# The place of every PSUM tile written in the source: a table of banks in place of two buffer counts

## The chip, the core and the metric

The kernel runs on one core of one Trainium2 chip. The number that counts is its time on the device in microseconds (us); three runs of the kernel before are at hand, and their median is the time to which the changed kernel is compared. Beside them stands one execution taken by the hardware profiler, with a row for every instruction of five engines: TensorE (PE in the profile, its weight loads apart as PEld), VectorE (DVE), ScalarE (ACT), GpSimd (POOL) and SyncE (SP), which issues the DMAs. "Span" is the time from the first to the last instruction of that execution.

## What is computed

A linear-attention recurrence with a decay per channel, and behind it a feed-forward layer with the larger of two projections. Cut to what matters:

```python
# r, k, v, w: (4, 8, 768, 48);  u: (8, 48)
for t in range(S):
    cur = einsum('bhd,bhe->bhde', u[None] * kt, vt)
    y[:, :, t] = einsum('bhd,bhde->bhe', rt, state + cur)
    state = wt[:, :, :, None] * state + einsum('bhd,bhe->bhde', kt, vt)
x = y.transpose(0, 2, 1, 3).reshape(3072, 384)
g = maximum(x @ w1, x @ w2)          # 384 -> 1024
out = g @ w_out                      # 1024 -> 384, float32
```

## The kernel before

**Tiling.** The 768 steps are cut into three segments of 256 tokens, and the eight units are batches of such segments: units 0 to 3 are one batch each of the first segment, units 4 and 5 two batches each of the second, 6 and 7 two batches each of the third. Inside a segment the recurrence becomes matrix products: a key-query score tile for each of two halves, masked, times the values; the state that a segment leaves is carried into the next.

**Order.** Nothing is scheduled by a tool. A string `ORDER` lists 652 short steps, each naming a function, its unit and parts, and after an `@` the engine; the kernel walks through it and records each step's instructions. Every engine then runs its own instructions in that order, and an instruction starts when those ahead of it on its engine have been issued and the semaphores that it waits for have been raised. A wait at the head of an engine's queue holds back all that is behind it.

**The steps that matter here.** In a step's name the first number is the unit.

- `sc` (function `sc`, matmuls at L641): scores of a batch and half, into a pair of PSUM banks. `mk` (L650, VectorE) reads them through the mask into the bf16 tile `M`.
- `ya` (L688) and `yi` (L675): masked scores times values, and state times queries, summed into one pair for a batch. `xe` (copy helper at L168) takes that pair out to `xT`.
- `kv` (L596): the segment's new state, into a pair; `st` (L612, L615, VectorE) reads it. It needs `kp` from `scale` (multiplications by the helpers L176 on VectorE, L180 on GpSimd) and `vp` from `vb` (L168).
- `ex` (L395 to L398): prefix sums of the logarithms, into a bank; `e0` (L436, ScalarE) takes the exponential in place, and `scale` reads it. `ie` (L460, ScalarE) makes the inverse factors `iE`.
- `gt` (L706): one eighth of the 1024 hidden channels for a unit, into a bank; `rl` (L717 on ScalarE, L719 on VectorE) writes them out as `gT`.
- `op` (L725 for the folded part, L729 for the rest): 128 output rows into a bank; `oe` copies them out, `os` (L743) stores them.
- `dt` (L582): DMA transposes of `rp` and `kp` into `RK`, from which `sc` reads. `load` (L372): loads of r, k, v, w.

**PSUM.** It has eight banks of 2 KiB on each partition. Tag `G` has four of them (each tile one bank; 113 tiles in the program), tag `Y` has the other four as two pairs (44 tiles). Which of the four banks, or of the two pairs, a tile gets is left to the pool: it has a number of buffers for each tag and hands one out when the tile is made. The first write to a tile has to wait until the last reader of the tile that had the place before is done, so the place decides for whom TensorE waits.

```python
BANKS = {'G': 4, 'Y': 2}
```

Around the place of which most is said below, `ORDER` reads (units 4 to 7 mixed):

```
mz.6.1 e0.6.1 ie.6.0 kw.6.0@d e0.6.0 scale.6.1.1.0@p di.5.1@d sc.5.1.0.0
ya.5.0.1.0 rw.6.0@d ya.5.0.0.0 yi.5.0 xe.5.0@a vb.6.0@a scale.6.0.0.0@d op.4.2 wl.5 os.3.1
scale.6.1.0.0@p sc.5.1.1.0 oe.4.2@a op.4.0 oe.4.3@a oe.4.0@a mk.5.1.0.0 wp.7.0@p ya.5.1.0.0
mk.5.1.1.0 dt.6.0.0 ya.5.1.1.0 yi.5.1 kv.6 scale.6.0.1.0@d dt.6.0.1 xe.5.1@d st.6.0 dt.6.1.1 ln.7.0
```

## Time and profile before

| | before |
|---|---|
| three runs, us | 146.37, 147.02, 146.45 |
| their median, us | 146.45 |
| the profiled execution's span, us | 147.2 |
| mean granted TensorE clock in it | 0.987 |
| VectorE busy, us | 116.9 (79%) |
| ScalarE busy, us | 90.6 (62%) |
| GpSimd busy, us | 90.0 (61%) |

The profiled execution has no time of its own beside its span, and that span is longer than each of the three runs. Durations below are from this one execution. In rows of the timeline the first number is the start in us from the start of the span, the second the time from the first start to the last end of the merged instructions, then come engine, line, operation, the tile written and the tiles read; what stands in brackets is how long the engine was idle just before, and who ended that.

### The profile page before, as it was taken

The numbers are of one execution on the slowest core, as the hardware profiler recorded it, in microseconds if no ns is written. First come the engines' busy times: TensorE is split into PE (matmuls) and PEld (weight loads), VectorE is DVE, ScalarE is ACT, GpSimd is POOL, SyncE is SP. The second block draws the span as 40 slices with busy tenths as digits, with TensorE's granted clock in tenths as the row PEclk, the third lists the DMA queues.
The fourth block names the chain that finished last, engine by engine and source line by source line (L and its number), as shares of the span: only waits on it lengthen the run. The fifth ranks groups of instructions, "written<-read, shape, count | busy, mean of one in ns | idle before, by whom it ended". The sixth has DMA issues, their size and how long they took to land.

```text
span 147.2 us, 5536 instructions
## 1 busy us (share of the span) xinstructions
PE 136.8 (93%) x2403; PEld 84.2 (57%) x2404; DVE 116.9 (79%) x162; ACT 90.6 (62%) x164; POOL 90.0 (61%) x106
## 2 busy tenths in 40 slices
PE   5999999779999999999999994999999999999990
PEld 1355755568757666875654562554557545664560
DVE  2489999999999999999999967399967589361511
ACT  4053793997999849999178677367357483227010
POOL 7659979996986299499785909506996900000000
PEclk9999999999999999999999999599999999999999
DMA  4999999999899899997978999799933990051014
GB/s 104 323 325 357 335 401 394 366 286 304 214 241 277 212 226 282 312 255 174 205 192 177 292 251 207 141 138 291 250 136 78 131 271 20 0 210 62 4 56 157
DMA packets 71186, 31.84 MB, mean 216 GB/s; under 512 B 66293, under 2 KB 70390, under 8 KB 71162
## 3 DMA queue, kind: packets, MB, share of 16 engines
q1 hardware_dynamic: 71162, 31.49, 81.2%
q8 instruction: 19, 0.31, 0.8%
q14 instruction: 5, 0.04, 0.2%
HBM read 23.61 MB, written 4.73 MB: 193 GB/s over the span
## 4 chain that ended last, share of the span: by engine, by line
PE 41%; DVE 35%; issue 6%; POOL 6%; DMA 4%; ACT 3%; SPq 2%; DVEq 0%; POOLq 0%; ACTq 0%
PE G L729 12%; DVE M L650 9%; PE G L706 8%; PE G L234 7%; PE G L725 5%; DVE rp L176 4%; DMA lv<-in_v_dram 4%; DVE rku L176 3%; DVE dg L502 3%; POOL kp L180 3%; DVE M L516 3%; PE Y L688 2%; SPq L582 2%; POOL rku L180 2%; PE Y L675 2%
## 5 line engine op out<-in xcount | busy, mean ns | idle before, releaser
L729 PE MATMUL G<-wo_sb,gT 128*128 128x384 bf16 x192 | 35.8, 331 | 0.0
L706 PE MATMUL G<-xT,wd_sb 128*128 128x256 bf16 (+1 forms) x192 | 34.4, 326 | 0.7 <-ACT xT L168 0.6
L650 DVE CAST_PREDICATED M<-mask,Y 128x1024 bf16<-128x1024 int32 (+1 forms) x26 | 28.6, 1131 | 2.8 <-PE Y L641 1.9
L717 ACT ACTIVATE gT<-G 128x512 bf16<-128x512 f32 x43 | 24.5, 601 | 9.8 <-PE G L706 9.6
L729 PEld LDWEIGHTS <-gT 128*128 128x128 bf16 x192 | 19.0, 99 | 12.6 <-issue 0.3
L706 PEld LDWEIGHTS <-wd_sb 128*128 128x128 bf16 x192 | 17.9, 98 | 12.6 <-DVE wd_sb L176 0.6
L180 POOL TENSOR_TENSOR kp<-lk,iE 128x384 bf16<-128x384 f32 x16 | 17.1, 1096 | 9.3 <-DVE lk L176 4.2
L725 PE MATMUL G<-wc_sb,xT 128*128 128x384 bf16 x72 | 15.7, 327 | 0.0
L180 POOL TENSOR_TENSOR rku<-rku,u_b 128x384 f32<-128x384 f32 x14 | 14.5, 1053 | 2.0 <-DVE rku L176 2.0
L234 PE MATMUL G<-S_b 128*128 128x512 bf16 x47 | 13.6, 442 | 1.8 <-DVE S_b L263 1.8
L168 ACT COPY RK<-G 128x1024 bf16<-128x1024 bf16 x12 | 12.1, 1019 | 4.7 <-PE G L565 4.7
L168 ACT COPY osb<-G 128x384 f32<-128x384 f32 x7 | 3.4, 479 | 15.9 <-PE G L729 12.6
L180 POOL TENSOR_TENSOR rku<-lr,lk 128x384 f32<-128x384 f32 x8 | 10.9, 1393 | 2.5 <-DMA lk<-in_k_dram 1.7
L641 PE MATMUL Y<-RK 48*64 48x128 bf16 x384 | 9.0, 220 | 2.6 <-DVE M L650 2.4
L502 DVE TENSOR_REDUCE dg<-rku 128x16 f32<-128x768 f32 x12 | 11.0, 945 | 0.1
L641 PEld LDWEIGHTS <-RK 48*64 48x64 bf16 x384 | 6.2, 106 | 7.8 <-issue 6.7
L168 ACT CAST xT<-Y 128x768 bf16<-128x768 f32 x7 | 7.0, 1025 | 5.3 <-PE Y L675 4.0
L168 ACT CAST S_b<-S_f 64x768 bf16<-64x768 f32 (+1 forms) x14 | 8.7, 624 | 2.3 <-DVE S_f L612 2.0
L176 DVE TENSOR_TENSOR rp<-lr,G 128x768 bf16<-128x768 f32 (+2 forms) x11 | 8.8, 799 | 1.4 <-ACT G L436 1.4
L234 PEld LDWEIGHTS <-S_b 128*128 128x128 bf16 x48 | 5.1, 112 | 8.3 <-issue 3.3
L516 DVE TENSOR_TENSOR M<-identq,gd 128x512 int32<-128x512 int32 x12 | 9.2, 778 | 0.4 <-POOL gd L168 0.3
L168 DVE CAST xT<-Y 128x768 bf16<-128x768 f32 x5 | 5.1, 1017 | 5.5 <-PE Y L688 3.2
(111 smaller groups left out, 240.2 us busy)
## 6 DMA issues: line engine op xcount, KB each, us to landing
lk<-in_k_dram SPq DMA_DIRECT2D x12, 384.0 KB, 4.7
lv<-in_v_dram SPq DMA_DIRECT2D x12, 384.0 KB, 5.8
lr<-in_r_dram SPq DMA_DIRECT2D x10, 384.0 KB, 5.5
lw<-in_w_dram SPq DMA_DIRECT2D x9, 384.0 KB, 5.4
out_dram<-osb SPq DMA_DIRECT2D x14, 192.0 KB, 3.9
gT<-in_moe_w_dram SPq DMA_DIRECT2D x4, 512.0 KB, 8.3
out_dram<-wb SPq DMA_DIRECT2D x10, 192.0 KB, 2.0
wso<-in_moe_w_out_dram SPq DMA_DIRECT2D x4, 384.0 KB, 5.5
```

What stands on the lines that cost most here:

```text
L168: (nc.scalar.copy if e == "a" else nc.vector.tensor_copy if e == "d" else nc.gpsimd.tensor_copy)(o, i)
L176: op(o, a, b)
L180: op(o[:, g], a[:, g], b[:, g])
L234: nc.tensor.matmul(t, zz[:, 0:P], zz[:, 0:512], start=True, stop=True)
L502: nc.vector.reduce_sum(s.dg[:, b].rearrange("p i h -> p h i"), s.rku[:, b], axis=AX.X)
L516: (nc.vector if en == "d" else nc.gpsimd).tensor_tensor(out=o, in0=m, in1=g.unsqueeze(3).to_broadcast([P, 2, H, Q // 2]), op=ALU.bitwise_and)
L641: nc.tensor.matmul(t[q * Q:(q + 1) * Q, e, p * P:(p + 1) * P].rearrange("s (i g) -> s i g", i=2), s.kT[d, b, j, y * n + p, q, :], s.rT[d, ...
L650: nc.vector.copy_predicated(t[:, :, 2 * n * y:2 * n * (y + 1)].rearrange("s i (p e) g -> s p e i g", e=2), mask[:, j].bitcast(I32).unsquee ...
L706: nc.tensor.matmul(t[:, m * n * P:(m + 1) * n * P].rearrange("c (b t) -> c b t", t=P), wd_sb[:, ko, fo * P:(fo + 1) * P], s.xT[:, 0:n, ko, :],
L717: nc.scalar.activation(o, i, AF.Relu)
L725: nc.tensor.matmul(t[:, 0:HD], s.xT[:, a, ko, :], wc_sb[:, ko, :], start=(ko == 0), stop=False)
L729: nc.tensor.matmul(t[:, 0:HD], s.gT[:, c:c + P], wo_sb[:, f, :], start=False, stop=(f == FO - 1))
```

## The change

The two buffer counts go, and a table takes their place: one digit for each tile, in the order in which the tiles are made. A digit says which of four banks (`G`) or of two pairs (`Y`) the tile gets, by making the tag `G0` to `G3` or `Y0`, `Y1`, each with a single buffer. By the table, a new tile gets the place whose last user stands earliest in `ORDER`. No step, no instruction and no engine's order is changed; the source grows by nine lines above the steps, so each line number after them is larger by nine.

```diff
-BANKS = {'G': 4, 'Y': 2}
+PLACES = {
+    'G': ("0123013112032303031020230130230210323102121320123013021021023120121310231013021321302131"
...
+    'Y': ("01001010010101010110010010011010101101011001"),
+}
...
+    places = {tag: iter(x) for tag, x in PLACES.items()}
+
+    def place(tag):
+        return tag + next(places[tag])
+
     def bank(dt=F32, tag="G"):
-        return ps.tile([P, 512 if dt is F32 else 1024], dt, tag=tag, name=tag, bufs=BANKS[tag])
+        return ps.tile([P, 512 if dt is F32 else 1024], dt, tag=place(tag), name=tag, bufs=1)

     def pair(tag="Y"):
-        return ps.tile([P, 2, 512], F32, tag=tag, name=tag, bufs=BANKS[tag])
+        return ps.tile([P, 2, 512], F32, tag=place(tag), name=tag, bufs=1)
```

Names of banks aside, most tiles follow the same tile as before on their place. Another one goes before them at 21 of the 157 tiles. Four of these are pairs: `sc.5.0.1.0` and `kv.5`, then `sc.5.1.1.0` and `ya.5.1.0.0`. The seventeen banks are those of `gt.1.3`, `gt.0.2`, `gt.0.3`, `ex.3.0`, `gt.3.0`, `gt.2.3`, `op.3.0`, `op.3.1`, `gt.5.4`, `gt.5.6`, `gt.6.5`, `gt.6.3`, `gt.6.6`, `gt.6.0`, `gt.6.1`, `op.6.0` and `op.6.2`. In the built program the only thing that moves is for whom TensorE's instructions wait (and one instruction of ScalarE waits for a later one of its own engine, ahead of it in the same queue).

The first place is on TensorE, unit 5 and the output of unit 4: `Y_2196` is the pair of `sc.5.1.1.0`, `G_2215` the bank of `op.4.0`, `Y_2235` the pair of `ya.5.1.0.0`. Before:

```order
L729 MATMUL G_2179<-wo_sb_87,gT_1870 128x384
L641 LDWEIGHTS RK_1678
L641 MATMUL Y_2196<-RK_1678 64x128 [waits DVE_49]
...
L725 LDWEIGHTS xT_1815
L725 MATMUL G_2215<-wc_sb_88,xT_1815 128x384 [waits Activation_49]
...
L688 LDWEIGHTS vp0_76
L688 MATMUL Y_2235<-M1_81,vp0_76 32x128 [waits Activation_49]
```

The same place of the changed program:

```order
L738 MATMUL G_2179<-wo_sb_87,gT_1870 128x384
L650 LDWEIGHTS RK_1678
L650 MATMUL Y_2196<-RK_1678 64x128 [waits Activation_49]
...
L734 LDWEIGHTS xT_1815
L734 MATMUL G_2215<-wc_sb_88,xT_1815 128x384 [waits DVE_49]
...
L697 LDWEIGHTS vp0_76
L697 MATMUL Y_2235<-M1_81,vp0_76 32x128 [waits DVE_49]
```

`sc.5.1.1.0` had the pair of `sc.5.1.0.0` and so waited for VectorE's `mk.5.1.0.0`; it now has the pair of `ya.5.0` and waits for ScalarE's `xe.5.0`. `op.4.0` keeps the bank of `ex.6.0` and its wait for VectorE's `scale.6.0.0.0`, which the wait ahead of it had covered, now stands at itself. `ya.5.1.0.0` has changed pairs the other way and waits for `mk.5.1.0.0`, whose result it reads in any case.

The second place is on TensorE, hidden channels of unit 6: `G_2841`, `G_2845`, `G_2852` are the banks of `gt.6.6`, `gt.6.0`, `gt.6.1`, and `G_2914` that of `op.6.0`. Before:

```order
L706 MATMUL G_2841<-xT_2741,wd_sb_86 128x512 [waits DVE_49]
...
L706 MATMUL G_2845<-xT_2741,wd_sb_86 128x512 [waits Activation_49]
...
L706 MATMUL G_2852<-xT_2741,wd_sb_86 128x512 [waits Activation_49]
...
L725 MATMUL G_2914<-wc_sb_88,xT_2741 128x384 [waits DVE_49]
L725 LDWEIGHTS xT_2741
```

In the changed program:

```order
L715 MATMUL G_2841<-xT_2741,wd_sb_86 128x512 [waits Activation_49]
...
L715 MATMUL G_2845<-xT_2741,wd_sb_86 128x512 [waits Activation_49]
...
L715 MATMUL G_2852<-xT_2741,wd_sb_86 128x512 [waits DVE_49]
...
L734 MATMUL G_2914<-wc_sb_88,xT_2741 128x384 [waits Activation_49]
L734 LDWEIGHTS xT_2741
```

`gt.6.6` follows `gt.6.3` on its bank in place of the prefix sums of unit 7, and so waits for ScalarE's `rl.6.3`; `gt.6.0` follows `gt.6.5` in place of `gt.6.3`; `gt.6.1` takes the bank that the prefix sums had; `op.6.0` follows `gt.6.7` in place of `gt.6.0`, which VectorE had read.

## The prediction

> **What bounds the kernel now.** First the page of the profiled execution: the share of each engine, the TensorE clock in 40 slices, and the chain of work that ended last.

> ```profile
> span 147.2 us, 5536 instructions
> ...
> PE 136.8 (93%) x2403; PEld 84.2 (57%) x2404; DVE 116.9 (79%) x162; ACT 90.6 (62%) x164; POOL 90.0 (61%) x106
> ...
> PE   5999999779999999999999994999999999999990
> ...
> PEclk9999999999999999999999999599999999999999
> ...
> PE 41%; DVE 35%; issue 6%; POOL 6%; DMA 4%; ACT 3%; SPq 2%; DVEq 0%; POOLq 0%; ACTq 0%
> ```

> TensorE is busy for 93% of the span. Inside the kernel one slice of 3.7 us stands at 4 tenths, the 25th, and in the next the clock falls to 5 tenths. The change touches nothing but TensorE's waits, so the next view is who TensorE waited for (total us, times, longest).

> ```profile
> PE Y L641 <- DVE M L650: 2.4, 3, 1.9
> PE G L234 <- DVE S_b L263: 1.8, 1, 1.8
> ...
> PE Y L688 <- DVE M L650: 0.2, 1, 0.2
> ```

> Only the first row is a wait for a place in PSUM: scores (L641) do not read what the mask step (L650) writes, they wait for the pair that it reads. One such wait is 1.9 us; the two others share 0.5. No row has a write to a `G` bank waiting for its reader `gT` or `osb`. The chain in order of time says whether the 1.9 us count (start, us, what).

> ```profile
> 89.51 1.15 DVE M L650
> 90.70 0.42 PE Y L641 x16
> ...
> 117.13 0.56 DVE S_f L612
> ...
> 123.48 0.42 PE Y L641 x16
> ...
> 143.87 0.56 DVE wb L168
> ```

> They do: from 90.70 the chain is TensorE alone up to 117.1, then VectorE waits for it there, and from 123.48 it is TensorE to the last output copy. What is gained at 90.70 reaches the end unless something else comes due between.

> **Part 1, the wait of `sc.5.1.1.0`.** The timeline around it; in brackets the idle time before.

> ```profile
> 85.66 0.75 PE L688 MATMUL Y<-M,vp 64*32 64x128 bf16 x64
> 86.33 0.53 PE L675 MATMUL Y<-RK,S_b 128*32 128x128 bf16 x24
> 86.79 0.66 PE L725 MATMUL G<-wc_sb,xT 128*128 128x384 bf16 x3
> 88.22 3.87 POOL L180 TENSOR_TENSOR kp<-lk,iE 128x384 bf16<-128x384 f32 x4 [3.90 <-ACT iE L460]
> 88.46 1.01 ACT L168 CAST xT<-Y 128x768 bf16<-128x768 f32 x1
> 88.55 0.95 DVE L176 TENSOR_TENSOR rp<-lr,G 128x768 bf16<-128x768 f32 x1 [1.37 <-ACT G L436]
> 88.68 0.10 PEld L641 LDWEIGHTS <-RK 48*64 48x64 bf16 x1 [0.32 <-issue]
> 89.43 1.22 DVE L650 CAST_PREDICATED M<-mask,Y 128x1024 bf16<-128x1024 int32 x1
> 90.70 0.42 PE L641 MATMUL Y<-RK 48*64 48x128 bf16 x16 [1.94 <-DVE M L650]
> 91.05 0.66 PE L725 MATMUL G<-wc_sb,xT 128*128 128x384 bf16 x3
> 93.64 1.06 PE L688 MATMUL Y<-M,vp 64*32 64x128 bf16 x64
> 94.63 0.84 PE L675 MATMUL Y<-RK,S_b 128*32 128x128 bf16 x24
> 95.40 0.74 PE L596 MATMUL Y<-vp,kp 64*64 64x48 bf16 x32
> 96.07 0.66 PE L725 MATMUL G<-wc_sb,xT 128*128 128x384 bf16 x3
> 97.87 0.38 PE L706 MATMUL G<-xT,wd_sb 128*128 128x512 bf16 x1
> ```

> The mask step ends at 89.43 + 1.22 = 90.65, and the scores start 0.05 later. Now they wait for `xe.5.0`, the copy to `xT` on ScalarE, which ends at 88.46 + 1.01 = 89.47; with the same 0.05 they start at 89.52. That takes off **1.18 us** of the 1.94. Nothing else holds them: the weight load at 88.68, which reads the same `RK`, had already gone. What is next late? `op.4.0` needs the bank that the `rp` step frees at 89.50; it would come at 89.87. The product of masked scores (L688) reads both mask steps; the second followed the scores and now follows the first mask step directly, at about 90.65 to 91.87, while TensorE comes to its half of the product only around 92.0. `kv.6` (L596) reads `kp`, ready on GpSimd at 88.22 + 3.87 = 92.09, and would come at 95.40 − 1.18 = 94.2, or at 92.8 with part 2. So the whole 1.18 goes on.

> **Part 2, the clock.** The same stretch in windows (TensorE busy first, the granted clock behind the five engines).

> ```profile
> 88.70:92.10 3.40, 1.46 (x24) 1.01 (x24) 2.88 (x3) 2.22 (x4) 3.40 (x5) 1.00 0.88 191
> 92.10:95.60 3.50, 3.50 (x102) 2.07 (x102) 1.21 (x3) 1.22 (x2) 1.91 (x2) 0.51 0.75 144
> ```

> After 3.4 us in which TensorE was busy for 1.46, it got half the clock for about as long. No other stretch inside the kernel has either. The price is read from equal work at full clock: `op.4.0` takes 93.64 − 91.05 = 2.59 against 97.87 − 96.07 = 1.80 for `op.4.1`; the product of unit 5's second batch 94.63 − 93.64 = 0.99 against 86.33 − 85.66 = 0.67 for the first; the state's part 95.40 − 94.63 = 0.77 against 86.79 − 86.33 = 0.46. That is 0.79 + 0.32 + 0.31 = **1.42 us**. With the pause cut to 0.76, such a window is busy for some 2.6 us of 3.4. The row nearest to that is on the page: the 8th and 9th slice of TensorE stand at 7 tenths, and the clock stays at 9 there. So I take the drop as gone; the other end is that it stays, and gives nothing.

> [...]

> **Part 3, what then comes due.** 1.18 + 1.42 = 2.60 would be the shift at 96.07. The next engine that does not move as far is GpSimd, which makes `kp` and `vp` for `kv.7`.

> ```profile
> 95.98 1.97 SPq L372 DMA_DIRECT2D lr<-in_r_dram  x2
> 100.79 4.97 POOL L180 TENSOR_TENSOR rku<-lr,lk 128x384 f32<-128x384 f32 x4 [0.80 <-POOL gd L168]
> 109.14 1.95 POOL L180 TENSOR_TENSOR lk<-lk,lw 128x384 f32<-128x384 f32 x2
> 111.27 0.84 ACT L460 ACTIVATE iE<-MZ 128x768 f32<-128x768 f32 x1 [1.45 <-DVE MZ L440]
> 112.24 2.73 POOL L180 TENSOR_TENSOR kp<-lk,iE 128x384 bf16<-128x384 f32 x2 [1.15 <-issue]
> 114.91 0.83 POOL L168 CAST vp<-lv 128x768 bf16<-128x768 f32 x1
> 116.40 0.69 PE L596 MATMUL Y<-vp,kp 64*64 64x48 bf16 x32
> ```

> From 100.79 GpSimd works without a break to 111.09, idles 1.15 until `iE` is there, and ends at 115.74; `kv.7` starts at 116.40. `iE` comes from TensorE's prefix sums and moves with it, so the 1.15 can go; TensorE's own room is 116.40 − 115.74 = 0.66. The start at 100.79 hangs on the load of r issued at 95.98, which stands in SyncE's queue behind the transposes of unit 6. These start after VectorE's `scale.6.0.1.0`, which follows the second mask step and moves by 0.52, from 91.16 to about 90.65. If the load lands 0.52 earlier the limit is 0.66 + 1.15 + 0.52 = 2.3; if it lands when it did, 1.8. I take 2.1 between them, as both ends are near.

> Behind that VectorE's run from 117.13 begins with a wait for `kv.7` and moves with it.

> **Part 4, the other places.** None of them has a row in the list above, which goes down to 0.2 us, so each can give 0 to 0.2; I take 0, since the waits that the list does name for these matmuls are others. What they can cost is a wait where slack shrinks; the tightest are in unit 6.

> ```profile
> 115.86 1.08 ACT L717 ACTIVATE gT<-G 128x512 bf16<-128x512 f32 x2 [1.19 <-PE G L706]
> 117.02 2.76 PE L706 MATMUL G<-xT,wd_sb 128*128 128x512 bf16 x12
> 117.88 1.09 ACT L717 ACTIVATE gT<-G 128x512 bf16<-128x512 f32 x2 [0.93 <-PE G L706]
> ```

> `gt.6.6` at 117.02 now waits for the first of the two copies from 115.86, over at about 116.4, which is 0.6 before. `gt.6.0` comes a tile later (2.76 us for four tiles, so 0.65 or so, at 117.7) and waits for the second, over at 116.94, which is 0.7 before. ScalarE itself waits for TensorE there (1.19 and 0.93), so both move together: 0.

> **Sum.** In the profiled execution 147.2 − 2.1 = **145.1**. This execution has no time beside its span, and the span is 0.75 over the median of the runs. I read the 0.75 as chance, most simply as a clock drop that not every run has in full; the changed kernel has none, so 145.1 stands as a time.

> **The rivals.**

> *The runs' median has no clock drop.* Then the drop is no gain there: before is already 1.42 earlier from 96 on, and the limit of 2.1 leaves 0.7: 146.45 − 0.7 = 145.75. For it: 146.37 and 146.45 against 147.02 and a span of 147.2 look like two kinds. Against: with 1.42 the two kinds should lie further apart.

> *The span is longer than a time by a fixed 0.75.* Then 146.45 − 2.1 = 144.35. Three runs, one of them at 147.02, speak neither way.

> *The clock drop stays.* The halving has another cause than the pause, and part 1 is all: 147.2 − 1.2 = 146.0. The halved 3.4 us right behind the only long pause speak against it, and nothing in the profile names another cause. [...]

> *The change does not do what it says.* The scores start no earlier, because the copy to `xT` is itself late in most executions: it stands on ScalarE behind the cast of `vp`, which waits for a load. Then 146.45. The weight load at 88.68 and the row of the copy speak against it.

> *Slower: ScalarE falls behind in unit 6's hidden channels.* Its point is 0.6 us late at `gt.6.6`; from there each microsecond late is one of TensorE's. Late by 2.5 it makes a pause of 1.9, and with the drop of 1.42 behind it 3.3: 145.1 + 3.3 = 148.4. ScalarE's idle 1.19 and 0.93 just there speak against it.

> **How the numbers follow.** Forecast 0.42; median without a drop 0.22; fixed offset 0.12; drop stays 0.12; nothing 0.08; slower 0.04. The likeliest time is 145.1. From 144.2 to 146.1 all but the last two cases lie, which leaves a little out at the edges for the two ends of the limit. A measurement of this kernel can tell about 0.5% from no change, 0.73 us, so faster means under 145.7: the forecast, the offset, half of the median's case and half of the staying drop, 0.42 + 0.12 + 0.11 + 0.06 = 0.71. Within it: the other halves and nothing, 0.25. Slower: 0.04.

> **What would show it.** Right: the row of scores `Y L641` behind `DVE M L650` falls from 2.4 to about 0.5 in TensorE's waits; a pause of about 0.8 before these scores, ended by ScalarE's `xT`; no slice with a clock under 9 before the last; `kv.7` waiting for GpSimd's `vp`, or just not. Wrong: a pause of 1.9 still there with another releaser; the clock halved all the same after a pause of 0.8; TensorE waiting for `gT` in unit 6. What would make it wrong most simply is a median that never had the drop.

## The result and the profile after

| | before | changed |
|---|---|---|
| median, us (runs) | 146.53 (7) | 145.44 (7) |
| lowest to highest, us | 145.94 to 147.03 | 145.36 to 146.32 |
| span of the profiled execution, us | 147.2 | 143.6 |
| mean granted TensorE clock in it | 0.987 | 1.000 |

The ratio is 0.9937 with a 95% interval of 0.9913 to 0.9962, so the changed kernel is 0.4 to 0.9% faster. The two spans differ by 3.6 us, the medians by 1.1: the two profiled executions differ by more than the change. The runs of the changed kernel have spans listed beside their times, and the time is 1.7 to 1.8 us above the span in each (145.40 and 143.6; 146.32 and 144.5). By that the execution profiled before, with its span of 147.2, took about 149.0 us, and none of the seven runs before was as long.

The page of the profile after, the same lines as before:

```profile
span 143.6 us, 5537 instructions
...
PE 135.7 (94%) x2403; PEld 83.7 (58%) x2404; DVE 116.3 (81%) x162; ACT 90.7 (63%) x164; POOL 89.5 (62%) x106
...
PE   5999989798999999999999999999999999999990
...
PEclk9999999999999999999999999999999999999999
...
PE 81%; DVE 14%; issue 2%; ACT 1%; DVEq 0%
```

The 25th slice, which stood at 4 tenths, is at 9, the clock does not fall, and the share of VectorE in the chain has gone from 35% to 14%. TensorE's waits (total us, times, longest), the whole list:

```profile
PE G L243 <- DVE S_b L272: 1.8, 1, 1.8
PE G L574 <- DVE rp L185: 0.8, 2, 0.5
PE G L715 <- ACT xT L177: 0.6, 1, 0.6
PE Y L605 <- DVE M L659: 0.4, 1, 0.4
PE G L316 <- ACT wb L177: 0.3, 1, 0.3
PE Y L650 <- DVE M L659: 0.2, 1, 0.2
PE G L574 <- ACT RK L177: 0.2, 1, 0.2
PE Y L697 <- DVE M L659: 0.2, 1, 0.2
```

The scores behind the mask step, 2.4 us before, are down to 0.2, and no other row has come in for them: no bank waits for `gT`. The timeline at the place of the old pause (line numbers are larger by nine):

```profile
85.03 0.83 ACT L177 CAST vp<-lv 128x768 bf16<-128x768 f32 x1
85.17 0.42 PE L650 MATMUL Y<-RK 48*64 48x128 bf16 x16
87.15 1.46 PE L738 MATMUL G<-wo_sb,gT 128*128 128x384 bf16 x8
87.31 1.02 ACT L177 CAST xT<-Y 128x768 bf16<-128x768 f32 x1
88.28 2.35 DVE L659 CAST_PREDICATED M<-mask,Y 128x1024 bf16<-128x1024 int32 x2
88.55 0.42 PE L650 MATMUL Y<-RK 48*64 48x128 bf16 x16
```

The scores start at 88.55, without a pause: the copy to `xT` that they wait for ended at 87.31 + 1.02 = 88.33, ahead of TensorE's work in front of them. The two mask steps follow each other without a break. But not all of this is the change: the cast of `vp`, which needs a load of v, did not wait for it here, and in the execution profiled before it did:

```profile
85.31 0.42 PE L641 MATMUL Y<-RK 48*64 48x128 bf16 x16
86.17 0.83 ACT L168 CAST vp<-lv 128x768 bf16<-128x768 f32 x1 [0.90 <-DMA lv<-in_v_dram]
```

The scores in these rows, of `sc.5.1.0.0`, serve as a mark: the cast starts 0.14 us ahead of them in the profile after (85.03 against 85.17) and 0.86 behind them in that of before, so the load was about 1.0 us late there.

### The profile page after: what moved, and what is told of

Same layout as the page of the kernel before. It is cut to its first block, busy times and chain, and to the rows that moved or that the text cites. A ratio compares the mean times of both kernels' runs of the same rounds, so it can differ in the third digit from the quotient of the medians.

```text
span 143.6 us, 5537 instructions
## 1 busy us (share of the span) xinstructions
PE 135.7 (94%) x2403; PEld 83.7 (58%) x2404; DVE 116.3 (81%) x162; ACT 90.7 (63%) x164; POOL 89.5 (62%) x106
## 4 chain that ended last, share of the span: by engine, by line
PE 81%; DVE 14%; issue 2%; ACT 1%; DVEq 0%
PE G L738 21%; PE G L715 20%; PE G L734 9%; PE G L243 7%; PE Y L697 5%; DVE M L659 4%; PE Y L650 4%; PE Y L684 3%; PE G L327 3%; PE Y L605 2%; PE G L574 2%; DVE M L525 2%; DVE dg L511 2%; DVE rp L185 1%; PE G L475 1%
## 5 line engine op out<-in xcount | busy, mean ns | idle before, releaser
L738 PE MATMUL G<-wo_sb,gT 128*128 128x384 bf16 x192 | 35.1, 326 | 0.0
L396 ACT ACTIVATE lg<-lg 128x768 f32<-128x768 f32 (+2 forms) x9 | 5.7, 628 | 7.0 <-DVE lg L185 5.4
L650 PE MATMUL Y<-RK 48*64 48x128 bf16 x384 | 9.0, 220 | 0.3 <-DVE M L659 0.2
L650 PEld LDWEIGHTS <-RK 48*64 48x64 bf16 x384 | 6.1, 106 | 5.4 <-issue 4.8
L185 DVE TENSOR_TENSOR rku<-lr,lk 128x768 f32<-128x768 f32 x6 | 6.4, 1061 | 3.5 <-DMA lr<-in_r_dram 3.5
```

Source lines behind the costliest of these rows:

```text
L185: op(o, a, b)
L650: nc.tensor.matmul(t[q * Q:(q + 1) * Q, e, p * P:(p + 1) * P].rearrange("s (i g) -> s i g", i=2), s.kT[d, b, j, y * n + p, q, :], s.rT[d, ...
L738: nc.tensor.matmul(t[:, 0:HD], s.gT[:, c:c + P], wo_sb[:, f, :], start=False, stop=(f == FO - 1))
```

## Experiments

**The same table with the old places.** The table names the places that the pool had given, so that every wait is the old one.

```diff
-    'G': ("0123013112032303031020230130230210323102121320123013021021023120121310231013021321302131"
-           "2102013020132130213201320"),
-    'Y': ("01001010010101010110010010011010101101011001"),
+    'G': ("0123013112032303031020203103023013202130101203102132103103120321323031203130213013021303"
+          "1231032013023021102130213"),
+    'Y': ("01001010010101010110010101101010101101011001"),
```

> The table with the places that the pool gave before; every wait is as before. Theory (the gain is one wait, that of sc.5.1.1.0): same as before, 0 +- 0.2 us, with a pause of TensorE of about 1 us ahead of sc.5.1.1.0, ended by VectorE's mask step, and a clock that is halved in some executions. Rival (single-buffer tags or the table themselves help): about 1 us faster than before.

Measured: 146.76 us against 146.56, ratio 1.0003 (0.9976 to 1.003). Its timeline, at the pause:

```profile
85.28 0.42 PE L650 MATMUL Y<-RK 48*64 48x128 bf16 x16
85.67 0.83 ACT L177 CAST vp<-lv 128x768 bf16<-128x768 f32 x1 [0.43 <-DMA lv<-in_v_dram]
88.92 1.22 DVE L659 CAST_PREDICATED M<-mask,Y 128x1024 bf16<-128x1024 int32 x1
90.19 0.42 PE L650 MATMUL Y<-RK 48*64 48x128 bf16 x16 [1.47 <-DVE M L659]
```

The tags alone do nothing that the interval would show. The pause is there, 1.47 us long in this execution. Its cast of `vp` starts 0.39 us behind the marking scores, later than in the profile after and earlier than in that of before.

**Only the pairs, and only the banks.** Each takes one row of the table from the old places and the other from the new. For the pairs alone, the table with the old places becomes (for the banks alone, its `G` rows become the new ones instead):

```diff
-    'Y': ("01001010010101010110010101101010101101011001"),
+    'Y': ("01001010010101010110010010011010101101011001"),
```

> Banks as before, the 44 pairs by the new table: three waits differ from before, those of sc.5.1.1.0, op.4.0 and ya.5.1.0.0. Theory: the whole gain, 0.9 to 1.1 us faster than before, no pause of over 0.5 us ahead of sc.5.1.1.0, full clock in nearly every run. Rival (the gain is spread over the seventeen banks): about half of it or less.

> Banks by the new table, pairs as before: 17 waits differ from before, that of sc.5.1.1.0 is the old one. Theory: same as before within 0.2 us, the pause of about 1 us ahead of sc.5.1.1.0 is there. Rival: half of the gain or more, 0.5 us or more faster.

The changed kernel itself ran beside them on the same chip.

> The changed kernel, beside the three others on one chip. Theory: 0.9 to 1.1 us faster than before, and equal to the kernel with the new pairs alone. Rival: faster than that one by what the banks add.

Measured, each against the same 29 runs of before (median 146.56):

| kernel | median, us | ratio | interval |
|---|---|---|---|
| places as before | 146.76 | 1.0003 | 0.9976 to 1.003 |
| pairs alone | 145.47 | 0.9927 | 0.9898 to 0.9955 |
| banks alone | 146.42 | 0.9995 | 0.9974 to 1.0017 |
| the change | 145.37 | 0.9926 | 0.9898 to 0.9953 |

Within these intervals the three waits that the pairs alter, those of `sc.5.1.1.0`, `op.4.0` and `ya.5.1.0.0`, are the whole gain, and the seventeen banks add none: the change and the pairs alone are 0.1 us apart. Of the three, only the wait of `sc.5.1.1.0` shows as time in which TensorE was idle. The timeline with the banks alone:

```profile
84.87 0.83 ACT L177 CAST vp<-lv 128x768 bf16<-128x768 f32 x1
85.00 0.42 PE L650 MATMUL Y<-RK 48*64 48x128 bf16 x16
88.11 1.22 DVE L659 CAST_PREDICATED M<-mask,Y 128x1024 bf16<-128x1024 int32 x1
89.39 0.42 PE L650 MATMUL Y<-RK 48*64 48x128 bf16 x16 [0.94 <-DVE M L659]
```

Here the load of v was in time: no wait stands ahead of the cast, which starts 0.13 us ahead of the marking scores, and the pause is 0.94 us. Against this the cast was 0.52 us late with the places as before and 0.99 late in the profile of before, and the pauses there are longer by 0.53 and 1.00: the pause grows by as much as the load is late. The load was in time in eight of the ten profiled executions of all kernels in this text, so 0.94 is the pause in an ordinary one. It is about the gain: 0.7% of 146.56 is 1.1, and 0.6% in the first comparison 0.9. With the pairs alone the pause is gone:

```profile
87.27 1.01 ACT L177 CAST xT<-Y 128x768 bf16<-128x768 f32 x1
88.66 0.42 PE L650 MATMUL Y<-RK 48*64 48x128 bf16 x16
```

The clock is full there (1.000). Of the 53 executions with the old pairs in this comparison (before, places as before, banks alone) three had a mean clock under 0.99, and they were each one's longest, 148.69 to 149.28 us; of the 25 with the new pairs, the first comparison's among them, none had. So the half clock of the profile before is a rare companion of the old places, and too rare to set a median. With the new places two of the changed kernel's twelve executions here were longer too, 146.49 and 146.97 us at full clock (1.000); what made them so is not shown.

**ScalarE made late.** To see the case that the prediction worked out, ScalarE is held up by copies of a constant onto itself, just ahead of `e0.6.1`, with the old places and with the new.

```diff
-load.7.w.0 load.7.k mz.6.1 e0.6.1 ie.6.0 kw.6.0@d e0.6.0 scale.6.1.1.0@p di.5.1@d sc.5.1.0.0
+load.7.w.0 load.7.k mz.6.1 lag.4@a e0.6.1 ie.6.0 kw.6.0@d e0.6.0 scale.6.1.1.0@p di.5.1@d sc.5.1.0.0
...
+    def c_lag(n, e):
+        for _ in range(n):
+            copy(e, tri, tri)
...
```

> Places as before, and four ScalarE copies of the constant tri onto itself ahead of e0.6.1: ScalarE, and behind it VectorE's mask step, is late by their time (about 1.2 us), as it is when the load of v lands late. Theory (a long pause halves the clock): a pause of about 2.1 us ahead of sc.5.1.1.0, ended by the mask step; the clock halved for 3.4 us behind it in some runs; 1.2 us slower than before in runs without that, 2.6 us in runs with it. Rival (the half clock of the profile of before had nothing to do with the pause): full clock in every run, 1.2 us slower in all.

> The changed kernel with the same four copies: this is the case that the prediction worked out (the load late, the new pair). Theory: sc.5.1.1.0 waits about 1.0 us for the copy to xT, full clock in every run; 1.2 to 2.6 us faster than the old places with the same copies, as 1.2 us of wait go and, where it was there, the half clock (1.4). Rival (a limit at kv.7 on GpSimd, as in the prediction's third part): the difference stays under 1.2 us.

The timeline of the old places with four copies, then its windows (TensorE's busy time first, the granted clock behind the five engines):

```profile
85.06 0.83 ACT L177 CAST vp<-lv 128x768 bf16<-128x768 f32 x1
85.79 1.28 ACT L177 COPY tri<-tri 128x128 f32<-128x128 f32 x4
89.49 1.22 DVE L663 CAST_PREDICATED M<-mask,Y 128x1024 bf16<-128x1024 int32 x1
90.76 0.42 PE L654 MATMUL Y<-RK 48*64 48x128 bf16 x16 [2.13 <-DVE M L663]
91.61 2.77 PE L742 MATMUL G<-wo_sb,gT 128*128 128x384 bf16 x8
100.46 5.42 POOL L189 TENSOR_TENSOR rku<-lr,lk 128x384 f32<-128x384 f32 x4 [0.21 <-POOL gd L177]
109.25 1.95 POOL L189 TENSOR_TENSOR lk<-lk,lw 128x384 f32<-128x384 f32 x2
112.45 2.74 POOL L189 TENSOR_TENSOR kp<-lk,iE 128x384 bf16<-128x384 f32 x2 [1.25 <-issue]
116.61 0.69 PE L609 MATMUL Y<-vp,kp 64*64 64x48 bf16 x32
```

```profile
88.10:91.60 3.50, 1.37 (x23) 0.76 (x21) 2.46 (x3) 2.88 (x6) 3.31 (x4) 1.00 0.97 213
91.60:95.10 3.50, 3.50 (x74) 1.86 (x71) 1.71 (x2) 0.69 (x2) 2.48 (x3) 0.51 0.37 71
```

And the new places with the same copies:

```profile
85.52 0.83 ACT L177 CAST vp<-lv 128x768 bf16<-128x768 f32 x1
88.98 1.01 ACT L177 CAST xT<-Y 128x768 bf16<-128x768 f32 x1
90.05 0.42 PE L654 MATMUL Y<-RK 48*64 48x128 bf16 x16 [0.95 <-ACT xT L177]
90.89 1.46 PE L742 MATMUL G<-wo_sb,gT 128*128 128x384 bf16 x8
100.18 5.10 POOL L189 TENSOR_TENSOR rku<-lr,lk 128x384 f32<-128x384 f32 x4 [2.15 <-issue]
107.95 1.97 POOL L189 TENSOR_TENSOR lk<-lk,lw 128x384 f32<-128x384 f32 x2
110.21 2.74 POOL L189 TENSOR_TENSOR kp<-lk,iE 128x384 bf16<-128x384 f32 x2 [0.29 <-POOL lk L189]
112.89 0.82 POOL L177 CAST vp<-lv 128x768 bf16<-128x768 f32 x1
114.37 0.69 PE L609 MATMUL Y<-vp,kp 64*64 64x48 bf16 x32
```

The pause goes from 2.13 to 0.95, by 1.18 us, and changes its releaser from VectorE's mask to ScalarE's `xT`. The eight matmuls behind the scores take 2.77 us at the half clock and 1.46 with the new places. By the mean clock (0.974 to 0.988) the old places had the half clock in four of four executions, the new ones in none of ten (0.996 and more). The old places' four executions took 149.05, 149.34, 149.76 and 152.01 us, the last with the lowest clock; the median of the other three is 149.34, and that of the new places 146.46. The ratios to before are 1.0198 (1.0161 to 1.0236) and 1.0007 (0.9978 to 1.0036). Before had 13 executions beside these, of which one took 193.28 us at a mean clock of 0.662; its cause is not known, and it is outside the ratios. So the difference is 2.8 to 2.9 us, just over the upper end of what was expected, and the rival with a limit under 1.2 falls.

> Places as before, eight copies (about 2.4 us): Theory: a pause of about 3.3 us ahead of sc.5.1.1.0 and the clock halved behind it in every run; about 3.8 us slower than before. Rival (no tie between pause and clock): 2.4 us slower.

> The changed kernel with eight copies: sc.5.1.1.0 waits about 2.2 us for the copy to xT. Theory: as long a pause as in the profile of before, so the clock halved in some runs or in most; 1.2 us faster than the old places with eight copies where both are halved, 2.6 us where only the old is. Rival (the clock goes by another engine's wait): never halved here.

With the old places and eight copies, the scores in the timeline, and the windows around their pause:

```profile
92.06 0.64 PE L654 MATMUL Y<-RK 48*64 48x128 bf16 x16 [3.44 <-DVE M L663]
```

```profile
88.20:91.70 3.50, 0.42 (x3) 0.13 (x2) 1.78 (x2) 3.50 (x7) 2.11 (x3) 1.00 0.43 90
91.70:95.10 3.40, 3.04 (x24) 1.59 (x24) 2.39 (x3) 0.59 (x2) 3.40 (x4) 0.50 0.40 77
```

The same two views with the new places:

```profile
91.49 0.42 PE L654 MATMUL Y<-RK 48*64 48x128 bf16 x16 [2.27 <-ACT xT L177]
```

```profile
89.60:93.10 3.50, 1.61 (x24) 1.05 (x24) 2.59 (x3) 3.28 (x6) 2.92 (x4) 1.00 0.57 118
93.10:96.50 3.40, 3.40 (x132) 2.37 (x130) 2.99 (x5) 0.96 (x2) 2.88 (x4) 1.00 0.74 97
```

Medians 150.33 and 148.67, ratios 1.0237 (1.0169 to 1.0305) and 1.0149 (1.0115 to 1.0183): 1.7 us apart, and the pauses of the two profiles 1.17. By its ratio the first is 3.5 us slower than before; 3.8 was expected. By the mean clock (0.986 to 0.989 against 1.000) it was halved in three of four executions with the old places and, at 0.988 against 1.000, in two of four with the new. "In every run" was too much, "in some" was right; the last section shows what goes with it. The rival without a tie between pause and clock falls: the new places, too, get the half clock in some executions once they are held up this long. (The profiled one, with a pause of 2.27, was not among them.) How the times add up here is in part open: at full clock the old places' 148.93 is only 0.5 to 0.6 above the new places' 148.31 and 148.40, and not 1.2, while those with the half clock lie 1.3 to 1.6 apart. Executions differ by as much before this place: where the load is in time, the cast of `vp` starts anywhere from 84.77 to 85.63. With so few executions of each kind, that can hide part of a difference.

## Why the prediction came out

**The number is right, and partly by two errors that cancel.** 145.1 was forecast, 145.44 measured, and the direction and size hold: one wait, that of `sc.5.1.1.0`, is the whole gain. But 145.1 was worked out from the profiled execution with its half clock and late load, by the step "I read the 0.75 as chance ... so 145.1 stands as a time". In that execution the forecast gain of 2.1 would lead to about 149.0 − 2.1 = 146.9. Its span was not 0.75 above a usual time; it was about 2.4 us over a usual execution, as a time is 1.7 to 1.8 us above its span. Taken together, the base was 0.7 us above the median of the runs before (147.2 against 146.53), and the gain 1.0 above the measured one (2.1 against 1.1). That the two nearly cancel is luck. A span longer than every time should have been the warning: where what lies around it adds time (1.7 to 1.8 us in each run of the changed kernel), it says that the execution shown is not a usual one.

**Part 1, the wait.** The mechanism is right, and in the conditions of that profile the size too: 1.18 forecast, 2.13 − 0.95 = 1.18 measured with ScalarE held up. In ordinary executions the load of v lands about a microsecond earlier, the pause is 0.94, and all of it goes, since `xe.5.0` is done before TensorE gets there. So the gain is 0.9 to 1.1 rather than 1.18 plus a clock term. One reading of the list of waits was incomplete: TensorE's new state, `kv`, also waits 0.4 us for a mask step whose tile it does not read, by that list a second wait for a place. It is there in the list after as well (L605), so the table does not remove every such wait.

**Part 2, the clock.** The tie between pause and half clock is borne out, by the pauses of 1.94 and 2.13 us and the half clock behind both. The price is borne out with the old places: with eight copies the one execution with a full clock took 148.93, the other three 150.26 to 150.52, which is 1.3 to 1.6 more (1.42 was forecast). With the new places and eight copies the two with the half clock took 148.94 and 148.99 against 148.31 and 148.40, only 0.5 to 0.7 more; they have no profile, so whether the price is smaller there stays open. What was wrong is to count the term into the gain of the median: three of 53 executions with the old pairs had it. The rival "the runs' median has no clock drop" is what happened. Its 145.75 was 0.3 too high, as it took only 0.7 of part 1's 1.18 because of the next part; with all of it, it would have said 145.27.

**Part 3, the limit at `kv.7`, was mis-sized.** It was put at 1.8 to 2.3 and the runs put it above 2.7. Between the two kernels with four copies `kv.7` moves from 116.61 to 114.37, by 2.24. But the profiled execution with the new places was 0.46 us behind before the copies (its cast of `vp` starts at 85.52 against 85.06), so the change is worth 2.70 there. GpSimd still idles 0.29 before `kp`, and from the end of its cast at 112.89 + 0.82 = 113.71 TensorE has 0.66 left, so the limit had not been reached.

The rows say where the 2.70 came from, with the 0.46 counted in. GpSimd's start on `rku` comes 0.74 earlier (100.46 against 100.18); the prediction had 0 to 0.52. Its idle time before `kp` falls from 1.25 to 0.29, by 0.96. And its work from the start of `rku` to the end of `lk` is 1.00 shorter: 10.74 us, from 100.46 to 111.20, against 9.74, from 100.18 to 109.92. This last term the prediction put at nothing, by taking the durations as they stood in one profile, where the same stretch is 10.3 us. It is 10.3 to 10.7 in the three profiles with the half clock and 9.2 to 9.8 in the other seven. Why is not shown.

**Part 4, the other places.** Right within the interval: banks alone give 0.9995 (0.9974 to 1.0017), and no wait for `gT` came up in unit 6, so the slower rival has no support. The rival that the change does not do what it says fell with the pairs alone.

**The pause and the half clock.** A pause of 1.94 us in the profile of before and one of 2.13 us with four copies were each followed by the half clock, and by the mean clock (0.974 to 0.988) all four executions of that kernel had it; with the new places and the same copies, at a pause of 0.95, none of ten had (0.996 and more). That speaks against the rival in which the halving has another cause than the pause.

## What to carry to other kernels

Where a few PSUM places are handed round, look up for each wait of a write who read the place last: giving the tile another place, with every instruction left where it is, took a wait of 0.94 us (the profile with the banks alone) off the critical path and was worth about as much to the end, 1.1 us by the medians. Before summing from one profiled execution, hold its span against the times, and its rare events (here a halved clock, in three of 53 executions with the old pairs, and a late load, in two of ten profiles) against whether the other runs can have had them. A limit taken from the summed durations of another engine in one profile is a wide range, since these durations differ between executions: here from 9.2 to 10.7 us for the same stretch of GpSimd.

## What was not expected of the hardware

```profile
87.80:91.20 3.40, 1.93 (x26) 1.10 (x25) 2.63 (x3) 2.62 (x5) 3.40 (x4) 1.00 0.94 209
91.20:94.60 3.40, 3.40 (x132) 2.42 (x130) 2.44 (x3) 1.32 (x2) 2.32 (x3) 1.00 1.10 139
```

So in these five executions a busy share of 0.43 or less of one such stretch was followed by the half clock, and one of 0.46 or more was not. The length of the pause alone does not sort them, since 1.94 us was followed by the half clock and 2.27 was not. The rest of the records agrees. The ten profiles have 405 stretches of this grid at full clock, the ends of the kernels among them: after each of the 13 with a share of 0.43 or less the clock was halved, and after none of the 392 with 0.46 or more. That the share in a fixed grid is what decides fits all of them, and the mixed outcomes of equal kernels; no run set the share by itself.
